# The low parts of w1 and w2 subtracted on VectorE instead of GpSimd, in a fused attention, gated product and soft mixture of experts

## The chip, the cores and the metric

One Trainium2 chip, one core of it. The time is that of one whole execution on the device in microseconds, as a median of runs. An execution with the hardware profiler is looked at beside it; its times are counted from the start of its span. The engines are TensorE (PE in the rows; PEld is its loading of weights), VectorE (DVE), ScalarE (ACT), GpSimd (POOL) and SyncE (SP, which issues most of the DMAs).

## The reference, cut to what matters

Attention with a causal mask and a decay bias over 32 heads of 576 tokens, a product of two projections in full precision, and a soft mixture of 8 experts. All inputs are float32.

```python
scores = scale * q @ k.T                      # 4 x 8 heads, 576 x 576, head_dim 64
scores = where(causal, -1e9, scores + minimum(bias, 0))   # bias from a cumulative sum of max(s, 0)
attn = exp(scores - max); attn /= sum(attn) + 1e-9
x = (attn @ v), heads side by side            # 2304 tokens x 512
a, b = x @ w1, x @ w2                         # w1, w2: 512 x 1024
x = (a * b @ w3) @ w_out                      # w3: 1024 x 1024, w_out: 1024 x 512
logits = x @ phi                              # 32 slots
slot_input = softmax over tokens(logits).T @ x
slot_out[e] = relu(slot_input[e] @ w1e[e]) @ w2e[e]
out = softmax over slots(logits) @ slot_out
```

## The kernel before, in words

The weights w1, w2, w3 and w_out come as 64-bit words of double precision and are turned into float32 on the chip. w1 and w2 together make eight tiles `w12t_0` to `w12t_7`, one for each block of 128 columns of the inner dimension; each comes in two halves of 512 words a partition (the names `w_w_5_1` and `raw_w_5_1` are the second half of tile 5). `fetch_words` has SP load a half into one of three buffers `raw` (L188). `load_words` then makes it a tile:

- ScalarE scales the high word (L202), VectorE shifts and ors in the sign and the low bits in three steps (L205, L206, L209). The last step, L209, is the last reader of the `raw` buffer, so the next SP load into that buffer waits for it.
- ScalarE rounds the float32 half to TensorE's reduced float32r (L233): the high part `th`. The difference between the value and its rounding is the low part `tl` (L234). A product with w1 or w2 is then the sum of three products of parts, `for wi, xi in ((0, 0), (0, 1), (1, 0))` at L457, so the matmuls of a block need both parts.

Around it, in the same stretch, runs the attention. For each head and tile of query rows TensorE makes scores in a PSUM buffer of the tag `sg` (L359; four such buffers, shared with the `gl` products of L457), VectorE adds the mask and takes the maximum (L362), ScalarE takes exponentials with their sum (L367), VectorE adds sums and inverts them (L376, L377), GpSimd scales the rows by the inverse (L380), TensorE transposes them (L395, L409) into PSUM buffers of the tag `tp` (two), ScalarE copies them out (L397, L411), TensorE multiplies with v (L110 with `x_ps`) and ScalarE and VectorE split the result into a rounded and a low part (L444, L445). As soon as x of a block is there, the `gl` products run, ScalarE copies one (L463) and VectorE multiplies it with the other (L475).

The order on the engines: the program is written as steps that `weave` mixes by costs, and a scheduler that simulates a timeline then lays out the instructions of TensorE, VectorE, ScalarE and GpSimd; each engine runs its own list in order. The order on SP stays as written. An operation that changes engine or length therefore changes the order around it, on all four engines.

Of the kernel before, what the change touches and what calls it, by code (L numbers as in the profile page):

```python
# [10 lines left out]
F32 = mybir.dt.float32  # L11
# [5 lines left out]
ALU = mybir.AluOpType  # L17
# [30 lines left out]
def attn_glu_softmoe_kernel(  # L48
# [14 lines left out]
    nc = tc.nc  # L63
# [127 lines left out]
    def convert(k, w, by_act, behind=None):  # L191
        raw = words.pop(k)
        pair = raw.bitcast(I32).rearrange("p (n t) -> p n t", t=2)
        hi, lo = pair[:, :, 1], pair[:, :, 0]
        wi, wu = w.bitcast(I32), w.bitcast(U32)
        order = mybir.DependencyInfo(mybir.DependencyClass.NoSync, mybir.DependencyReason.DATA)

        def line_up(step):
            if behind is not None:
                tc.add_manual_dep(step.ins, behind.ins.name, order, reason="order")  # L200

        line_up(nc.scalar.activation(out=w, in_=hi.bitcast(F32), func=AF.Copy, scale=F64_SCALE))  # L202
        lu = lo.bitcast(U32)
        if not by_act:
            nc.vector.tensor_scalar(out=wi, in0=wi, scalar1=3, scalar2=None, op0=ALU.logical_shift_left)  # L205
            nc.vector.scalar_tensor_tensor(  # L206
                out=wi, in0=hi, scalar=-0x80000000, in1=wi, op0=ALU.bitwise_and, op1=ALU.bitwise_or
            )
            return nc.vector.scalar_tensor_tensor(  # L209
                out=wu, in0=lu, scalar=29, in1=wu, op0=ALU.logical_shift_right, op1=ALU.bitwise_or  # L210
            )

        line_up(nc.scalar.activation(out=lo, in_=lu, func=AF.Copy, scale=LO_SCALE, bias=-0.49999))
        nc.vector.scalar_tensor_tensor(
            out=wi, in0=wi, scalar=3, in1=lo, op0=ALU.logical_shift_left, op1=ALU.bitwise_or
        )
        return nc.vector.scalar_tensor_tensor(
            out=wi, in0=hi, scalar=-0x80000000, in1=wi, op0=ALU.bitwise_and, op1=ALU.bitwise_or
        )
# [4 lines left out]
    def load_words(k, ap):  # L224
        (kind, i), e = TODO[k // 2], k % 2
        span = slice(512 * e, 512 * e + 512)
        if kind == "w12":
            if e == 0:
                w12_t[i] = wp.tile([P, 2, 2, KC, P], F32R, tag="W", name=f"w12t_{i}", bufs=NW)
            w = gq.tile([P, 512], F32, tag="g4", name=f"w_{kind}_{i}_{e}", bufs=NG4)  # L230
            convert(k, w, False)
            th, tl = (w12_t[i][:, n].rearrange("p a k f -> p (a k f)")[:, span] for n in range(2))
            nc.scalar.copy(out=th, in_=w)  # L233
            nc.gpsimd.tensor_tensor(out=tl, in0=w, in1=th.bitcast(F32), op=ALU.subtract)  # L234
        elif k < 2 * N0:
            if e == 0:
                rows_t[kind, i] = gq.tile([P, FC, P], F32, tag="g4", name=f"{kind}_{i}", bufs=NG4)
            rows_w[kind, i] = convert(k, rows_t[kind, i].rearrange("p c f -> p (c f)")[:, span], True)
        else:
            if e == 0:  # L240
                rows_t[kind, i] = ap.tile([P, 1024], F32, tag="words", name=f"w_{kind}_{i}", bufs=NRAW)
            convert(k, rows_t[kind, i][:, span], True, st["a_copy"])
# [514 lines left out]
    with tc.tile_pool(name="att", bufs=1) as ap:  # L757
# [11 lines left out]
            out=mask[:, S - P :], in_=mask[:, S - P :], pattern=[[-1, P]], base=0,  # L769
# [27 lines left out]
        def load(k):  # L797
            i = k // 2 - 1
            if FC <= i < N0:
                (sum_rows if k % 2 else use_rows)(*TODO[i])  # L800
            if k < 2 * N0:
                load_words(k, ap)
            if k + NRAW < 2 * N0:
                fetch_words(k + NRAW, ap)
# [10 lines left out]
        for i in range(N0, len(TODO)):  # L815
            more += [(1, lambda i=i: fetch_later(i)), (1, lambda: None)]
            more += [(1, lambda k=2 * i + e: load_words(k, ap)) for e in range(2)] + [(1, lambda: None)]
# [84 lines left out]
    for a in range(0, 4, 2):  # L902
        zt_ps = psum("tp", f"zt_ps_{a}")
        for c in range(2):
            nc.tensor.transpose(zt_ps[:, c * P : (c + 1) * P], z_acc[:, (a + c) * P : (a + c + 1) * P], ident)
        nc.vector.tensor_reduce(
            out=zt[:, a : a + 2], in_=zt_ps[:, : 2 * P].rearrange("p (c t s) -> p c s t", t=2, s=2 * NS),
# [233 lines left out]
```

## Time and profile before

| | us |
|---|---|
| runs without the profiler | 549.1, 550.09, 554.26 (median 550.09) |
| the profiled execution, its own time | 552.43 |
| its span, first to last instruction | 550.7 |
| TensorE busy in the span | 516.8 (94%) |
| VectorE, ScalarE, GpSimd busy | 329.0, 311.6, 130.6 |
| mean granted TensorE clock | 0.993 |

The profiled execution is 2.3 us above the median; 1.7 us of its time lie outside the span. A busy share says how much of a stretch an engine was inside an instruction, not that it was the limit there.

### The profile page before, as it was taken

What the parts mean: (1) busy time and instruction counts of PE and PEld (TensorE: products, weight loads), DVE (VectorE), ACT (ScalarE), POOL (GpSimd) and SP (SyncE); (2) the same over time, 40 slices, a digit from 0 to 9 for tenths busy, and PEclk for the clock granted to TensorE, in tenths of its full rate; (3) what the DMA queues carried; (4) which work ended last, traced back from release to release, by engine and by line L of the source; (5) the groups of instructions that cost most, each with busy time, mean ns of one, the idle gap of its engine ahead of it and who ended that gap; (6) DMA issues with size and microseconds to landing.
All of it is one profiled execution on the core that took longest, in us unless ns stands there. A gap on an engine that the chain in (4) does not pass through costs nothing.

```text
span 550.7 us, 11764 instructions
## 1 busy us (share of the span) xinstructions
PE 516.8 (94%) x4288; PEld 434.3 (79%) x4288; DVE 329.0 (60%) x1016; ACT 311.6 (57%) x845; POOL 130.6 (24%) x199
## 2 busy tenths in 40 slices
PE   2799899998999999999999999999999999989993
PEld 2567678877788898999989889899989999843452
DVE  7558787879987394866577668566630311252433
ACT  4567667687986674866577567558644211321222
POOL 4475563102454232110221311111310000000000
PEclk9999989999999999999999999999999999999998
DMA  5746973977673253563656537553514999689977
GB/s 147 235 146 193 280 223 128 292 259 269 218 253 102 73 161 113 169 201 133 194 170 211 173 99 208 176 172 114 167 44 137 413 411 376 241 293 423 420 295 241
DMA packets 38809, 118.03 MB, mean 214 GB/s; under 512 B 4224, under 2 KB 10560, under 8 KB 35296
## 3 DMA queue, kind: packets, MB, share of 16 engines
q1 hardware_dynamic: 36768, 113.60, 61.0%
q10 hardware_dynamic: 1984, 3.69, 2.4%
q8 instruction: 34, 0.56, 0.4%
q14 instruction: 23, 0.19, 0.1%
HBM read 102.11 MB, written 11.60 MB: 206 GB/s over the span
## 4 chain that ended last, share of the span: by engine, by line
PE 70%; DMA 13%; DVE 8%; ACT 4%; issue 2%; POOL 1%; SPq 0%; ACTq 0%; DVEq 0%; POOLq 0%
PE gl L457 31%; PE sc_ps L359 7%; PE x_ps L110 7%; PE pt_ps L395 5%; DMA raw_w<-in_w 5%; PE gn_ps L627 3%; PE o_ps L1042 3%; DMA raw_w3t<-in_w3t 3%; PE h_ps L1004 3%; PE ptd_ps L409 2%; PE z_ps L110 2%; DMA raw_wot<-in_wot 2%; DVE sc L362 1%; PE lg L110 1%; ACT sc L367 1%
## 5 line engine op out<-in xcount | busy, mean ns | idle before, releaser
L457 PE MATMUL gl<-x,w12t 128*128 128x320 f32 (+1 forms) x1536 | 237.7, 304 | 0.1
L457 PEld LDWEIGHTS gl<-x,w12t 128*128 128x128 f32 x1536 | 212.7, 190 | 7.4 <-issue 4.4
L380 POOL TENSOR_SCALAR sc<-sc,rinv 128x64 f32<-128x64 f32 (+4 forms) x160 | 101.1, 650 | 253.0 <-DVE rinv L377 85.7
L367 ACT ACTIVATE sc<-sc,nmax 128x64 f32<-128x64 f32 (+4 forms) x160 | 89.8, 563 | 31.4 <-DVE nmax L362 29.1
L362 DVE CUSTOM_DVE_ANT_0 sc<-sc_ps,mask 128x64 f32<-128x64 f32 (+4 forms) x160 | 65.0, 423 | 31.8 <-PE sc_ps L359 31.0
L397 ACT COPY pt<-pt_ps 128x128 f32<-128x128 f32 (+3 forms) x128 | 53.0, 426 | 34.1 <-PE pt_ps L395 25.1
L395 PE MATMUL pt_ps<-ident,sc 128*128 128x128 f32 x320 | 56.6, 286 | 5.5 <-POOL sc L380 3.2
L395 PEld LDWEIGHTS pt_ps<-ident,sc 128*128 128x128 f32 x320 | 38.4, 144 | 16.9 <-POOL sc L380 7.2
L463 ACT COPY a<-gl 128x256 f32<-128x256 f32 (+1 forms) x64 | 25.4, 398 | 46.0 <-PE gl L457 40.7
L359 PE MATMUL sc_ps<-qa 128*128 128x64 f32 (+1 forms) x144 | 46.4, 334 | 1.3 <-DVE gT L475 0.8
L110 PE MATMUL x_ps<-pt,v 128*64 128x256 f32 (+1 forms) x384 | 47.4, 358 | 0.0
L359 PE MATMUL sc_ps<-raw 68*128 68x288 f32 (+4 forms) x96 | 35.8, 516 | 11.6 <-DMA raw<-rows 9.8
L359 PE MATMUL sc_ps<-qb 68*128 68x64 f32 (+1 forms) x144 | 43.6, 306 | 0.9 <-DMA qb<-qa 0.9
L110 PEld LDWEIGHTS x_ps<-pt,v 128*64 128x64 f32 x384 | 33.5, 140 | 5.8 <-issue 1.0
L359 PEld LDWEIGHTS sc_ps<-raw 68*128 68x128 f32 x96 | 21.6, 265 | 16.9 <-issue 14.1
L202 ACT ACTIVATE w_w<-raw_w 128x512 f32<-128x512 f32 x32 | 21.6, 676 | 17.8 <-DMA raw_w<-in_w 17.7
L445 DVE TENSOR_TENSOR x<-x_ps,x 128x320 fp32r<-128x320 f32 (+1 forms) x32 | 14.1, 452 | 29.2 <-ACT x L444 29.2
L630 ACT COPY gn<-gn_ps 128x512 f32<-128x512 f32 x40 | 22.5, 584 | 15.5 <-PE gn_ps L627 15.1
L367 ACT ACTIVATION_READ_ACCUMULATOR sc<-sc,nmax 128x1 f32 x160 | 30.9, 193 | 0.0
L359 PEld LDWEIGHTS sc_ps<-qa 128*128 128x128 f32 x144 | 27.4, 190 | 3.6 <-DVE gT L475 1.3
L409 PE MATMUL ptd_ps<-ident,sc 128*128 128x128 f32 x160 | 25.9, 286 | 3.2 <-ACT pt L397 3.0
L359 PEld LDWEIGHTS sc_ps<-qb 68*128 68x128 f32 x144 | 27.4, 191 | 1.6 <-DVE v_sb L276 1.0
(180 smaller groups left out, 725.6 us busy)
## 6 DMA issues: line engine op xcount, KB each, us to landing
ew<-in_ew SPq DMA_DIRECT2D x27, 1024.0 KB
raw_w<-in_w SPq DMA_DIRECT2D x32, 512.0 KB
raw<-in_qk SPq DMA_DIRECT2D x24, 576.0 KB
v<-in_v SPq DMA_DIRECT2D x16, 576.0 KB
raw_w3t<-in_w3t SPq DMA_DIRECT2D x16, 512.0 KB
raw_wot<-in_wot SPq DMA_DIRECT2D x8, 512.0 KB
raw_wo<-in_wo SPq DMA_DIRECT2D x8, 512.0 KB
w_d<-w_w SPq DMA_DIRECT2D x8, 512.0 KB
```

The source lines that it names most:

```text
L110: mm = nc.tensor.matmul(out_, lhs, rhs, start=start, stop=stop)
L202: line_up(nc.scalar.activation(out=w, in_=hi.bitcast(F32), func=AF.Copy, scale=F64_SCALE))
L359: nc.tensor.matmul(pp[:r, : z - a], x[:, 0, q0 : q0 + r], x[:, 1, a:z], start=x is mul[0], stop=x is mul[-1])
L362: nc.vector.tensor_tensor_reduce(out=sc[:r, a:z], in0=pp[:r, : z - a], in1=hd["mask"][:r, m0 : m0 + z - a], scale=-0.125, scalar=3.0e38 if ...
L367: nc.scalar.activation(out=sc[:r, :W], in_=sc[:r, :W], func=AF.Exp, bias=nmax[:r, i : i + 1], scale=-1.0, accum_out=rsum[:r, i, 0:1],)
L380: nc.gpsimd.tensor_scalar(out=sc, in0=sc, scalar1=rinv[:, i : i + 1], scalar2=1.0, op0=ALU.mult, op1=ALU.mult)
L395: nc.tensor.transpose(tp[:, j * P : (j + 1) * P], sc[:, j * P : (j + 1) * P], ident)
L397: t["turned", i] = nc.scalar.copy(out=pt[:, p0 : p0 + step * (i - 1) + 1 : step], in_=tp[:, : i * P].rearrange("p (j q) -> p j q", q=P))
L409: nc.tensor.transpose(dg[:, p0 : p0 + P], t["sc"][:, c0 : c0 + P], ident)
L457: nc.tensor.matmul(acc[:, :nt], w12_t[fc][:, wi, n, kc], x_t[b, blk, kc][:, xi], start=k == 0, stop=k == 3 * KC - 1)
L463: st["a_copy"] = nc.scalar.copy(out=a_sb[:, :nt], in_=acc[:, :nt])
L630: st["turned", blk, k, h] = nc.scalar.copy(out=gn[:r, 4 * h : 4 * h + 4].rearrange("p c f -> p (c f)"), in_=tp[:r])
```

## The change

The sixteen subtractions of L234 are issued on VectorE instead of on GpSimd. Nothing else is written differently.

```diff
             nc.scalar.copy(out=th, in_=w)
-            nc.gpsimd.tensor_tensor(out=tl, in0=w, in1=th.bitcast(F32), op=ALU.subtract)
+            nc.vector.tensor_tensor(out=tl, in0=w, in1=th.bitcast(F32), op=ALU.subtract)
```

The scheduler lays the engines out anew. GpSimd's list goes from 201 to 185 rows and keeps the order of all the others; VectorE's goes from 993 to 1009, and its rows and those of TensorE and ScalarE are permuted in many places over the whole program. SP's list is the same.

On GpSimd, the piece of the difference around the scaling of the score tile `sc_802` (heads of the first batch, tiles of 448 and 576 columns):

```order
 L380 TENSOR_SCALAR sc_696<-sc_696,rinv_807 128x448
 L380 TENSOR_SCALAR sc_696<-sc_696,rinv_807 128x576
-L234 TENSOR_TENSOR w12t_761<-w_w_5_1_819,w12t_761 128x512
-L234 TENSOR_TENSOR w12t_879<-w_w_6_0_880,w12t_879 128x512
-L234 TENSOR_TENSOR w12t_879<-w_w_6_1_932,w12t_879 128x512
 L380 TENSOR_SCALAR sc_802<-sc_802,rinv_895 128x448
 L380 TENSOR_SCALAR sc_802<-sc_802,rinv_895 128x576
```

Three subtractions stood ahead of the scaling of `sc_802`; now nothing stands between it and the scaling before.

On VectorE, the same place of the program, before, from the product `gC_0_1` to the last step of the words of tile 7, first half:

```order
L475 TENSOR_TENSOR gC_0_1_841<-gl_0_1_1_828,a_0_1_784 128x320
L209 SCALAR_TENSOR_TENSOR w_w_6_1_932<-raw_w_6_1_769,w_w_6_1_932 128x512
L205 TENSOR_SCALAR w_w_7_0_988<-w_w_7_0_988 128x512
L376 TENSOR_REDUCE rinv_895<-rsum_95 128x2
L206 SCALAR_TENSOR_TENSOR w_w_7_0_988<-raw_w_7_0_826,w_w_7_0_988 128x512
L377 RECIPROCAL rinv_895<-rinv_895 128x2
L209 SCALAR_TENSOR_TENSOR w_w_7_0_988<-raw_w_7_0_826,w_w_7_0_988 128x512
```

And the changed kernel, from the same product on:

```order
L475 TENSOR_TENSOR gC_0_1_841<-gl_0_1_1_828,a_0_1_784 128x320
L234 TENSOR_TENSOR w12t_879<-w_w_6_0_880,w12t_879 128x512
L205 TENSOR_SCALAR w_w_7_0_988<-w_w_7_0_988 128x512
L206 SCALAR_TENSOR_TENSOR w_w_6_1_932<-raw_w_6_1_769,w_w_6_1_932 128x512
L376 TENSOR_REDUCE rinv_895<-rsum_95 128x2
L206 SCALAR_TENSOR_TENSOR w_w_7_0_988<-raw_w_7_0_826,w_w_7_0_988 128x512
L209 SCALAR_TENSOR_TENSOR w_w_6_1_932<-raw_w_6_1_769,w_w_6_1_932 128x512
L377 RECIPROCAL rinv_895<-rinv_895 128x2
L205 TENSOR_SCALAR w_w_7_1_1041<-w_w_7_1_1041 128x512
L445 TENSOR_TENSOR x_1_0_361<-x_ps_1_786,x_1_0_361 128x256
L209 SCALAR_TENSOR_TENSOR w_w_7_0_988<-raw_w_7_0_826,w_w_7_0_988 128x512
```

Between `gC_0_1` and the inversion of `rinv_895`, on which the scaling of `sc_802` waits, four rows stood before and six stand now, one of them a subtraction.

On VectorE, the piece of the difference at the last part of the scores `sc_696`, a few us earlier:

```order
 L362 ISA sc_696,nmax_695<-sc_ps_4_0_730,mask 128x288
 L362 ISA nmax_695 128x1
+L234 TENSOR_TENSOR w12t_664<-w_w_4_1_716,w12t_664 128x512
+L362 ISA sc_696,nmax_695<-sc_ps_4_1_733,mask,nmax_695 128x288
+L362 ISA nmax_695 128x1
 L205 TENSOR_SCALAR w_w_5_0_762<-w_w_5_0_762 128x512
 L206 SCALAR_TENSOR_TENSOR w_w_5_0_762<-raw_w_5_0_609,w_w_5_0_762 128x512
```

A subtraction now stands inside the score tile, between its last two parts (which have moved ahead of the words of tile 5). The rounding that it needs stands on ScalarE in the changed kernel here, behind two copies of transposes:

```order
L233 CAST w12t_664<-w_w_4_0_665 128x512
L411 COPY ptd_539<-ptd_ps_547 128x192
L397 COPY pt_588<-pt_ps_1_590 128x128
L397 COPY pt_588<-pt_ps_2_593 128x2x128
L233 CAST w12t_664<-w_w_4_1_716 128x512
```

The copy of `pt_ps_2_593` has moved ahead of this rounding; before, it stood behind it.

## Rows read from the trace of the kernel before

**Rows 1.** Stretches, core 0: start:end, length, busy us (count) by engine, PEclk, DMA, GB/s.

```profile
10.00:48.00 38.00, 33.16 (x127) 24.71 (x128) 22.76 (x92) 24.67 (x82) 19.27 (x30) 1.00 0.63 183
48.00:84.00 36.00, 32.63 (x216) 26.46 (x215) 30.43 (x66) 25.17 (x62) 22.58 (x18) 0.95 0.81 241
```

**Rows 2.** The same view in slices of 10 us, four of them.

```profile
70.00:80.00 10.00, 8.81 (x63) 7.17 (x62) 8.86 (x18) 6.47 (x14) 5.58 (x5) 0.95 0.73 221
80.00:90.00 10.00, 10.00 (x51) 8.38 (x51) 8.44 (x23) 9.37 (x21) 4.83 (x4) 0.88 0.40 132
...
140.00:150.00 10.00, 8.78 (x68) 7.24 (x68) 9.26 (x27) 9.19 (x27) 5.05 (x6) 1.00 0.62 199
...
200.00:210.00 10.00, 10.00 (x83) 9.43 (x84) 7.15 (x28) 6.45 (x22) 5.50 (x10) 1.00 0.58 181
```

**Rows 3.** Waits, 0 to 85 us: engine line <- releaser: us, times, longest.

```profile
POOL w12t L234 <- ACT w12t L233: 19.6, 6, 5.5
...
ACT w12t L233 <- DVE w_w L209: 6.1, 9, 1.5
...
PE pt_ps L395 <- POOL sc L380: 2.1, 2, 1.2
```

**Rows 4.** Stretches, the instructions of L234 on GpSimd alone: busy us (count).

```profile
10.00:48.00 38.00, 8.02 (x6) 1.00 0.63 183
48.00:84.00 36.00, 14.73 (x10) 0.95 0.81 241
```

**Rows 5.** The same view of L209 on VectorE alone.

```profile
48.00:84.00 36.00, 11.84 (x9) 0.95 0.81 241
```

**Rows 6.** The same view of L380 on GpSimd alone.

```profile
48.00:84.00 36.00, 8.01 (x8) 0.95 0.81 241
```

**Rows 7.** VectorE, L206: ns min/median/max, first and last start, shape.

```profile
L206 DVE SCALAR_TENSOR_TENSOR w_w<-raw_w,w_w x16: 672/694/1019, 8.1 to 78.4; 128x512 int32<-128x512 int32 x16
```

**Rows 8.** VectorE, L332, in the same view.

```profile
L332 DVE TENSOR_TENSOR qb<-raw,qa x24: 739/751/973, 99.9 to 380.1; 64x576 fp32r<-64x576 f32 x24
```

**Rows 9.** Timeline, 46 to 50 us: start, us, engine, line, [idle before <- releaser].

```profile
46.09 0.69 DVE L209 SCALAR_TENSOR_TENSOR w_w<-raw_w,w_w 128x512 uint32<-128x512 uint32 x1
...
48.00 1.66 POOL L234 TENSOR_TENSOR w12t<-w_w,w12t 128x512 fp32r<-128x512 f32 x1 [3.46 <-ACT w12t L233]
...
48.57 1.65 DVE L209 SCALAR_TENSOR_TENSOR w_w<-raw_w,w_w 128x512 uint32<-128x512 uint32 x1
```

**Rows 10.** Timeline, 73 to 80 us.

```profile
73.31 0.48 DVE L475 TENSOR_TENSOR gC<-gl,a 128x320 f32<-128x320 f32 x1
...
73.71 1.39 DVE L209 SCALAR_TENSOR_TENSOR w_w<-raw_w,w_w 128x512 uint32<-128x512 uint32 x1
...
75.02 0.41 DVE L205 TENSOR_SCALAR w_w<-w_w 128x512 int32<-128x512 int32 x1
...
75.36 0.15 DVE L376 TENSOR_REDUCE rinv<-rsum 128x2 f32<-128x4 f32 x1
...
75.83 1.46 POOL L234 TENSOR_TENSOR w12t<-w_w,w12t 128x512 fp32r<-128x512 f32 x1 [1.28 <-ACT w12t L233]
...
76.08 0.16 DVE L377 RECIPROCAL rinv<-rinv 128x2 f32<-128x2 f32 x1
...
77.27 2.48 POOL L380 TENSOR_SCALAR sc<-sc,rinv 128x448 f32<-128x448 f32 x2
...
78.66 0.68 PE L395 MATMUL pt_ps<-ident,sc 128*128 128x128 f32 x3 [1.19 <-POOL sc L380]
```

**Rows 11.** TensorE by line and shape, 10 to 45 us: count | busy us, mean ns.

```profile
L395 PE MATMUL pt_ps<-ident,sc 128*128 128x128 f32 x15 | 5.3, 439 | 0.9 <-POOL sc L380 0.9
```

**Rows 12.** The same group of the same view, 46 to 78 us.

```profile
L395 PE MATMUL pt_ps<-ident,sc 128*128 128x128 f32 x30 | 5.2, 283 | 1.9 <-ACT pt L397 1.9
```

## The prediction

> **What bounds the kernel now.** I read the stretches first. From about 80 us on TensorE is busy nearly all the time; the slice 200:210, with 10.00 of 10 busy, stands for most of what follows [rows 2]. The subtractions of L234 all lie before that, six in 10 to 48 us and ten in 48 to 84 us [rows 4]. So they can change the time only by how soon TensorE gets through its first 84 us: by its idle time there, 38 - 33.16 = 4.8 us in the first stretch and 36 - 32.63 = 3.4 us in the second [rows 1], and by its clock. The first 10 us are loads and decay rows and hold no subtraction.
>
> In both stretches I then look at who has room. VectorE is idle 38 - 22.76 = 15.2 us in the first but only 36 - 30.43 = 5.6 us in the second [rows 1]. That second stretch is where the change is decided; six operations more in the first are lost in its idle time.
>
> Last, the waits and the two timelines show how L234 bears on the others. GpSimd stood 19.6 us in six waits at the head of its list for the rounding on ScalarE [rows 3], and what was queued behind it, the scaling L380, waited along. And L234 slows VectorE: an L209 by itself took 0.69 us, the one that began 0.57 us into an L234 took 1.65 us and ended 0.56 us after that L234 did [rows 9].
>
> **What it removes.** GpSimd loses 8.02 + 14.73 = 22.75 us of work [rows 4]. Most of that is no gain: TensorE waited for the scaling only 2.1 us in two waits in this stretch [rows 3]. I price the larger. The inverse for `sc_802` ended at 76.08 + 0.16 = 76.24, but an L234 held GpSimd until 77.27, and TensorE began the transposes at 78.66 after 1.19 us idle [rows 10]. Without L234 the scaling could begin with the inverse, 1.03 us sooner, if the inverse came at the same time. It does not: between `gC_0_1` and the inverse VectorE now has a subtraction and two more steps of words. Counted from the end of gC at 73.79: 0.67 (L234, below) + 0.41 (L205) + 0.69 (L206) + 0.15 (L376) + 0.69 (L206) + 0.69 (L209, undisturbed) + 0.16 (L377) = 3.46 us, less about 0.08 us of overlap at each of seven borders (gC ran from 73.31 for 0.48, its follower began at 73.71), so 2.9 us, and the inverse is there at 76.7 [rows 7, 8, 10]. The scaling starts 0.6 us sooner: **-0.6 us**, with 0 and -1.0 as its ends.
>
> VectorE gets back the stretch of its own steps. The nine L209 in 48 to 84 us took 11.84 us, where nine of 0.69 would be 6.2: **5.6 us of VectorE's time** [rows 5, 9]. In the stretch before that there is nearly none. ScalarE's rounding waited 6.1 us in nine waits for L209 [rows 3], with copies of transposes behind it in its list; a part of the 5.6 comes out there. I take a tenth of it as TensorE's time, since TensorE's whole idle time in the stretch is 3.4 us and has several other causes: **-0.5 us**, ends 0 and -1.5.
>
> **What it adds.** Sixteen subtractions of two SBUF tensors on VectorE. The trace of before has no such row at 128x512. The nearest is L332, the same operation and output type at 576 columns: 751 ns, times 512/576 = 0.67 us. L206, two SBUF inputs at 512 columns, took 0.69 us as a median. I take 0.67 [rows 7, 8]. In 10 to 48 us that is 6 x 0.67 = 4.0 us into 15.2 us of idle time: nothing. In 48 to 84 us it is 10 x 0.67 = 6.7 us, against the 5.6 us that come back. VectorE is fuller there by 1.1 us out of 5.6 idle: **0 us**, with +1.1 as the end if all of it lands on the path. The cover is VectorE's idle time; should it be gone, every further us on VectorE delays L362 and the inverses, and TensorE with them.
>
> The subtraction still reads two SBUF tensors, and GpSimd still runs L380 in this stretch, 8.01 us of 36 in eight instructions of 1.0 us [rows 6]. If a subtraction meets one it can be held like that L209. At a share of 8.01/36 = 0.22 that is 10 x 0.22 x 1.0 = 2.2 us at most on VectorE, of which I leave 0 in the forecast for the idle time and keep +2.2 as an end. The Trainium skill (SBUF — State Buffer, Who interferes with whom) says that a VectorE instruction with two SBUF inputs and a GpSimd instruction that reads SBUF contend, and that whichever came later is blocked to the end of the other. The pair of rows with the 1.65 us agrees [rows 9]. By that rule moving the subtraction removes L209's opponent but leaves L380 as one for all four steps of a half; it is the second rival.
>
> What is moved is the one instruction, with no DMA of its own. New on VectorE is its wait for ScalarE's rounding. Queued behind it in the place inside `sc_696` is an L362, whose PSUM buffer TensorE needs again for scores or for gl; that is the first rival. SP's list does not change, and the loads that wait for L209 can go up to 0.6 us (5.6/9) sooner each, which I count as nothing because TensorE has its weights in time.
>
> **The sum.** -0.6 - 0.5 + 0 = -1.1 us. Against the profiled execution, 552.43 - 1.1 = 551.3. That execution lies 2.3 us above the median of 550.09; for the median I take 550.09 - 1.1 = **549.0 us**, no change that one would call one. A change of 1% is 5.5 us, about what a measurement of this kernel tells from none: its own three runs span 5.2 us.
>
> **The rivals.**
>
> *VectorE waits at the head of its list (slower).* The place: a subtraction between two parts of a score tile whose rounding stands behind copies of transposes on ScalarE, as in `sc_696`. GpSimd spent 19.6 us in six such waits, the longest 5.5 us [rows 3]; without it 14.1 us in five remain. VectorE comes to the subtraction with more work done ahead of it and waits less; half is 7 us. It decides once these waits exceed the 5.6 us of idle time. For it: L234 stands ahead of L362 in several places. Against: the scheduler has put other VectorE work between rounding and subtraction in most. 550.1 + 7 = 557 us.
>
> *The collision only changes partner (no change).* L380 blocks subtractions and L209 as priced: 1.1 + 2.2 = 3.3 us on VectorE, all of it on the path: 549.0 + 3.3 = 552.3 us. For it: GpSimd now runs its scalings as soon as the inverse is there, in the middle of VectorE's words.
>
> *TensorE's clock (faster).* The granted clock was 0.95 in 70:80 and 0.88 in 80:90 [rows 2]. Between the two levels of 1.2 and 2.4 GHz that is 1.0 + 2.4 us at the lower one, worth half: 1.7 us. The fall comes right behind the 1.19 us of idle time; if that shrinks the fall may go. Earlier, transposes occupied 5.3/15 = 0.35 us each in 10 to 45 us and 5.2/30 = 0.17 us in 46 to 78 us [rows 11, 12]: by their durations TensorE was at the lower level until about 45 us, though the granted clock in the row is 1.00 [rows 1]. TensorE's list is permuted in this stretch too. Were the rise to come 8 us sooner, up to 4 us of its work there would be saved, and as much lost the other way. With the fall gone and most of the 4 us: 549.0 - 1.7 - 3.3 = 544 us.
>
> *The later stretch is laid out anew.* Behind 110 us, as in 140:150 with TensorE at 8.78 and VectorE at 9.26 of 10 [rows 2], a new order can make waits or save them, some 2 us either way. It has no sign of its own.
>
> **How the numbers follow.** Forecast 0.57; the waiting VectorE 0.16; the changed partner 0.10; the clock 0.15; the later stretch 0.02. Faster by over 1% (below 544.6) takes the clock's case and a little: 0.17. Slower by over 1% (above 555.6) takes the first rival and a little: 0.17. Within 1%: 0.66. The range reaches down to the edge of the clock's case, 543.5, and up to where the first rival begins, 556.0; it holds the changed partner, and the spread of the runs of before.
>
> **What would show it.** Right, if the profile after has sixteen L234 on VectorE near 0.67 us, the nine L209 of the dense stretch near 0.69 us, the transposes of `sc_802` less than 1 us late, and TensorE idle 7 to 8 us between 10 and 84 us. The first rival would show as VectorE waiting for L233 by several us and TensorE waiting for PSUM behind L362. The second would show as L234 on VectorE well above 0.67 us beside an L380. The third would show in the granted clock between 70 and 90 us and in the durations of transposes before 45 us. I am wrong if TensorE's idle time in the first 84 us moves by more than 3 us.

## The result, and the profile after

The changed kernel takes 554.72 us (median of 8 runs, 554.15 to 558.01) against 550.99 for the kernel before (8 runs, 548.22 to 554.26): ratio 1.0077, 95% interval 1.0049 to 1.0105. It is slower by 0.8% (3.7 us between the medians, 4.2 by the ratio), where 1.1 us less was forecast. The profiled execution took 557.5 us with a span of 555.7, so it lies 2.8 us above its own median, as that of before lay 2.3 above its own at the time. All ratios and intervals are those on record, of undisturbed runs alone, and are not quotients of the two medians (here 1.0068), though close to them.

The instruction that moved does what was forecast. VectorE's rows of the line L234, which was GpSimd's [rows 4]; columns: ns min/median/max, first and last start, shape.

```profile
L234 DVE TENSOR_TENSOR w12t<-w_w,w12t x16: 679/688/1098, 12.1 to 93.9; 128x512 fp32r<-128x512 f32 x16
```

And L209, whose collision with L234 stood ahead [rows 5, 9], in the same view.

```profile
L209 DVE SCALAR_TENSOR_TENSOR w_w<-raw_w,w_w x16: 678/688/732, 9.9 to 88.8; 128x512 uint32<-128x512 uint32 x16
```

Sixteen subtractions at 0.69 us, one of them 1.10; no L209 above 0.73 where one took 1.65 before. GpSimd's work fell from 130.6 to 108.5 us, VectorE's grew from 329.0 to 332.0 only. The waits of the changed kernel from 0 to 85 us answer [rows 3]; columns: engine line <- releaser: us, times, longest.

```profile
ACT w_w L202 <- DMA raw_w<-in_w: 18.0, 12, 3.3
...
PE pt_ps L395 <- ACT ptd L411: 3.1, 2, 2.7
ACT w12t L233 <- DVE w_w L209: 3.0, 3, 1.4
...
PE pt_ps L395 <- POOL sc L380: 1.1, 1, 1.1
...
DVE w12t L234 <- ACT w12t L233: 0.8, 2, 0.6
```

VectorE waits 0.8 us for ScalarE's rounding where GpSimd had waited 19.6; ScalarE waits 3.0 us for L209 instead of 6.1; TensorE 1.1 us for the scaling instead of 2.1. Each of the three got better. What got worse is the first row: ScalarE's first step on the words, L202, waited 18.0 us in twelve waits for transfers, where the same view of the kernel before has nine:

```profile
ACT w_w L202 <- DMA raw_w<-in_w: 13.3, 9, 2.6
```

The stretches of the changed kernel, which answer [rows 1]; columns as there.

```profile
10.00:48.00 38.00, 32.86 (x120) 23.06 (x121) 26.71 (x99) 23.48 (x77) 13.84 (x24) 1.00 0.58 164
48.00:84.00 36.00, 31.04 (x168) 23.50 (x169) 22.25 (x58) 20.55 (x51) 4.24 (x6) 0.91 0.69 200
```

In 48 to 84 us TensorE was busy 1.6 us less than before, but got through 168 products instead of 216, and VectorE through 58 instructions instead of 66. VectorE's became shorter on average (0.38 us instead of 0.46), TensorE's longer (0.18 instead of 0.15; the mix of shapes differs): work comes later, and a part of TensorE's runs slower, as the timelines below show. Two slices answer [rows 2].

```profile
70.00:80.00 10.00, 7.27 (x31) 6.25 (x32) 6.97 (x17) 6.70 (x16) 0.81 (x1) 0.73 0.77 217
80.00:90.00 10.00, 10.00 (x68) 7.92 (x67) 8.52 (x20) 4.71 (x11) 2.31 (x2) 0.92 0.48 162
```

TensorE was idle 2.7 us in 70 to 80, and the clock granted there fell to 0.73, where it had been 0.95.

Where the delay begins is seen at TensorE's list. The kernel before, TensorE's timeline from 38 to 58 us: the `x_ps` row is the products of the second pair of heads (items 2 and 3; an item is one head with one block of its query rows), the `sc_ps` row the scores of item 8.

```profile
42.05 1.49 PE L110 MATMUL x_ps<-pt,v 128*64 128x256 f32 x7
...
44.37 2.10 PE L359 MATMUL sc_ps<-raw 68*128 68x448 f32 x6
```

The changed kernel, TensorE's timeline of the same stretch and of 60 to 84 us.

```profile
41.88 3.75 PE L359 MATMUL sc_ps<-raw 68*128 68x448 f32 x6 [0.57 <-DMA raw<-rows_d]
...
46.05 1.49 PE L110 MATMUL x_ps<-pt,v 128*64 128x256 f32 x8
...
69.87 0.71 PE L457 MATMUL gl<-x,w12t 128*128 128x320 f32 x3 [1.16 <-ACT x L444]
...
74.58 1.00 PE L395 MATMUL pt_ps<-ident,sc 128*128 128x128 f32 x4 [2.73 <-ACT ptd L411]
...
77.31 3.81 PE L457 MATMUL gl<-x,w12t 128*128 128x320 f32 x12
```

The scheduler, laying out the lists with sixteen VectorE instructions more, put the six products of item 8's scores ahead of the second pair's (and permuted much else). The same six took 3.75 us instead of 2.10: by that duration they now ran at the lower of TensorE's two levels, though the clock column reads 1.00 (last section). The pair came 4.0 us later. The two waits of 1.16 and 2.73 us come some 25 us after that.

SyncE's queue shows one link between the two. The kernel before, SyncE's timeline: the loads of v and the last load of words ahead of the first.

```profile
38.67 0.53 SPq L188 DMA_DIRECT2D raw_w<-in_w  x1
43.99 0.33 SPq L308 DMA_DIRECT2D v<-in_v  x1
...
52.76 0.33 SPq L308 DMA_DIRECT2D v<-in_v  x1
```

The same of the changed kernel.

```profile
38.97 0.53 SPq L188 DMA_DIRECT2D raw_w<-in_w  x1
48.01 0.33 SPq L308 DMA_DIRECT2D v<-in_v  x1
...
58.62 0.33 SPq L308 DMA_DIRECT2D v<-in_v  x1
```

There are two buffers for v. The load for items 6 and 7 needs the one that the second pair's products read last, so it goes out when they end, at 44.0 us before and 48.0 after. Eight loads of q, k, decay rows and words stand behind it in the same queue. In 4-us windows of the changed kernel (last columns: granted clock, DMA share, GB/s) the transfers cease:

```profile
44.00:48.00 4.00, 4.00 (x26) 2.62 (x25) 3.96 (x13) 2.05 (x5) 2.27 (x3) 1.00 0.00 0
...
56.00:60.00 4.00, 4.00 (x33) 3.02 (x33) 2.42 (x7) 2.43 (x7) 1.36 (x2) 1.00 0.13 31
```

The same windows of the kernel before:

```profile
44.00:48.00 4.00, 3.39 (x14) 2.30 (x15) 2.95 (x10) 3.06 (x9) 0.54 (x2) 1.00 0.65 179
...
56.00:60.00 4.00, 2.93 (x30) 2.24 (x30) 2.54 (x6) 1.38 (x4) 3.93 (x3) 1.00 0.92 293
```

The products of items 10 and 11, which I use as a mark below, began at 95.56 us instead of 90.36. TensorE's timeline of the kernel before:

```profile
90.36 1.51 PE L110 MATMUL x_ps<-pt,v 128*64 128x256 f32 x12
```

And of the changed kernel:

```profile
95.56 1.51 PE L110 MATMUL x_ps<-pt,v 128*64 128x256 f32 x12
```

The two profiled executions lie 5.1 us apart and the medians 3.7, so about 1 of these 5.2 us belongs to the executions and not to the change.

### The profile page after: what moved, and what is told of

Read it like the earlier page. It is cut to its first block, busy times and chain, and to the rows that moved or that the text cites. A ratio compares the mean times of both kernels' runs of the same rounds, so it can differ in the third digit from the quotient of the medians.

```text
span 555.7 us, 11755 instructions
## 1 busy us (share of the span) xinstructions
PE 522.6 (94%) x4288; PEld 436.7 (79%) x4288; DVE 332.0 (60%) x1032; ACT 312.2 (56%) x845; POOL 108.5 (20%) x183
## 4 chain that ended last, share of the span: by engine, by line
PE 78%; DMA 10%; DVE 7%; ACT 2%; issue 1%; SPq 1%; ACTq 0%; DVEq 0%
PE gl L457 35%; PE sc_ps L359 8%; PE x_ps L110 8%; DMA raw_w<-in_w 6%; PE pt_ps L395 6%; PE gn_ps L627 3%; PE ptd_ps L409 3%; PE o_ps L1042 3%; PE h_ps L1004 3%; PE z_ps L110 2%; DMA raw_w3t<-in_w3t 1%; PE lg L110 1%; DMA qb<-qa 1%; DVE sc L362 1%; PE y_ps L928 1%
## 5 line engine op out<-in xcount | busy, mean ns | idle before, releaser
L380 POOL TENSOR_SCALAR sc<-sc,rinv 128x64 f32<-128x64 f32 (+4 forms) x160 | 101.3, 652 | 299.0 <-DVE rinv L377 148.7
L359 PE MATMUL sc_ps<-raw 68*128 68x288 f32 (+4 forms) x96 | 40.5, 568 | 12.8 <-DMA raw<-rows 9.8
L359 PEld LDWEIGHTS sc_ps<-raw 68*128 68x128 f32 x96 | 23.0, 284 | 19.9 <-issue 15.3
L110 PEld LDWEIGHTS x_ps<-pt,v 128*64 128x64 f32 x384 | 31.9, 142 | 8.5 <-issue 2.9
L202 ACT ACTIVATE w_w<-raw_w 128x512 f32<-128x512 f32 x32 | 21.6, 677 | 20.4 <-DMA raw_w<-in_w 20.3
```

Source lines behind the costliest of these rows:

```text
L110: mm = nc.tensor.matmul(out_, lhs, rhs, start=start, stop=stop)
L359: nc.tensor.matmul(pp[:r, : z - a], x[:, 0, q0 : q0 + r], x[:, 1, a:z], start=x is mul[0], stop=x is mul[-1])
L380: nc.gpsimd.tensor_scalar(out=sc, in0=sc, scalar1=rinv[:, i : i + 1], scalar2=1.0, op0=ALU.mult, op1=ALU.mult)
```

## The experiments

To tell the order from the operation, most kernels carry the order of another. At the kernel's end a block adds order-only edges (an edge fixes which instruction comes first and adds no wait) between neighbours of a list; `LAY` holds the lists as numbers (cut here). What each experiment changes beside it is shown with it:

```diff
+    LAY = (
...
+    )
+    traced = list(nc.cur_bb.bb.instructions)
+    for row in json.loads(zlib.decompress(base64.b85decode(LAY))):
+        at, prev = 0, None
+        for d in row:
+            at += d
+            if prev is not None:
+                tc.add_manual_dep(traced[at], prev.name, order, reason="laid out")
+            prev = traced[at]
```

The table gives all kernels. The mark is the start of the products of items 10 and 11 (the row `x_ps<-pt,v 128x256 x12` near 90 us on TensorE) in the one profiled execution of each.

| kernel | median us (runs) | ratio to before | 95% interval | mark us |
|---|---|---|---|---|
| before | 550.99 (8) | 1 | | 90.36 |
| after | 554.72 (8) | 1.0077 | 1.0049 to 1.0105 | 95.56 |
| e1 VectorE, old order | 552.53 (12) | 1.0018 | 0.9986 to 1.0051 | 86.88 |
| e2 GpSimd, new order | 553.35 (12) | 1.0044 | 1.0014 to 1.0074 | 88.88 |
| e3 after, second pair first | 557.9 (6) | 1.0137 | 1.0096 to 1.0179 | 95.11 |
| e4 before, scores first | 558.68 (6) | 1.0128 | 1.0079 to 1.0177 | 94.74 |
| e5 VectorE, old head, new rest | 550.73 (12) | 0.9971 | 0.9947 to 0.9994 | 87.17 |
| e6 VectorE, new head, old rest | 557.85 (12) | 1.0073 | 1.0038 to 1.0108 | 92.59 |
| e7 after, more v | 549.27 (12) | 0.9943 | 0.9914 to 0.9973 | 88.73 |
| e8 before, more v | 549.0 (11) | 0.9956 | 0.9929 to 0.9982 | 86.19 |
| e9 after, ScalarE's list | 555.59 (8) | 1.0077 | 1.0049 to 1.0104 | 91.72 |
| e10 e4, more v | 552.52 (12) | 1.0008 | 0.9977 to 1.0039 | 89.14 |
| e11 e5, more v | 548.63 (12) | 0.9939 | 0.9915 to 0.9963 | 85.56 |
| e12 e5, subtracted twice | 556.63 (6) | 1.0092 | 1.0055 to 1.0128 | 93.14 |
| e13 after, v behind | 555.39 (12) | 1.0036 | 0.9992 to 1.0080 | 87.27 |
| e14 e12, more v | 554.47 (12) | 1.0045 | 1.0009 to 1.0081 | 93.00 |
| e15 e3, more v | 553.79 (12) | 1.0027 | 0.9997 to 1.0056 | 90.46 |
| e16 after, more v, laid anew | 556.75 (6) | 1.0118 | 1.0078 to 1.0157 | 95.80 |
| e17 before, more v, laid anew | 554.73 (6) | 1.0086 | 1.0053 to 1.0119 | 91.26 |

**e1 and e2: the operation or the order.** e1 is the changed kernel with the lists of TensorE, VectorE and ScalarE in the order of before (`LAY` is read from that kernel; the sixteen subtractions are free). e2 is the kernel before with the lists of the changed one.

> The subtraction on VectorE as in the changed kernel, but TensorE, VectorE, ScalarE and GpSimd keep the order of the kernel before, row for row; the sixteen subtractions are slotted in between VectorE's rows by the scheduler. Theory A (the loss is the permuted order, the operation itself costs nothing): 548 to 551 us, ratio to the kernel before 0.995 to 1.001, the v load of the third pair issued near 44 us and the transposes at full clock from about 46 us. Theory B (the time on VectorE costs, the order is innocent): 554 to 556 us, ratio 1.006 to 1.010, with waits of TensorE behind L362 or the inverses. Theory C (the clock of TensorE rises early or late by chance, neither matters): anything between, with runs as far apart as 5 us.

> The other way round: the subtraction on GpSimd as before, but TensorE, VectorE and ScalarE and the rest of GpSimd in the order of the changed kernel, row for row; the sixteen subtractions are slotted in between GpSimd's rows by the scheduler. Theory A: 554 to 557 us, ratio 1.006 to 1.012, the v load near 48 us and the clock of TensorE high only after 55 us. Theory B: 550 to 552 us, ratio 0.999 to 1.002. Theory C: anything between.

With the old order the subtraction on VectorE costs nothing that can be told from zero; with the new order the kernel is slower although GpSimd subtracts. The order costs. Both ratios fall between the bounds that theories A and B had set: e2 carries about half of the changed kernel's loss, and its interval reaches up to nearly all of it, so a part of the loss for the engine in the new order is not excluded.

**e3 and e4: one place in TensorE's list.** e4 moves the six products (three rows of the list, each of them two in a timeline) in the kernel before to where the changed kernel has them; e3 moves them back in the changed kernel. In short, by the names in the lists:

```diff
 e4: TensorE's list of the kernel before
+sc_ps_3_0_564 sc_ps_4_0_574 sc_ps_4_1_577   (six products, item 8)
 x_ps_0_392                                  (second pair)
-sc_ps_3_0_564 sc_ps_4_0_574 sc_ps_4_1_577
 e3: TensorE's list of the changed kernel
-sc_ps_3_0_564 sc_ps_4_0_574 sc_ps_4_1_577
 x_ps_0_392
+sc_ps_3_0_564 sc_ps_4_0_574 sc_ps_4_1_577
```

> The changed kernel with its own order on all engines, except that on TensorE the three score products of the first tile of the second block (sc_563) stand behind the product with v of the second pair of heads (x_ps_0_392) instead of ahead of it. Theory A in its narrow form (that one place delays the release of the v buffer, and SP's queue behind it): the v load is issued 1.5 to 2 us sooner than at 48.0, since the copy that the product needs ends near 43.9, and the time falls by 1.5 to 3 us, to 552 to 553 us. Theory A in its wide form (many small permutations): 554 to 555 us. Theory B: 554.7 us, unchanged.

> The kernel before with its own order on all engines, except that on TensorE the same three score products stand ahead of the product with v of the second pair, as they do in the changed kernel. Theory A, narrow: the v load moves from 44.0 to 46 us or later, and the time rises by 1.5 to 4 us, to 552.5 to 555 us. Theory A, wide: 551 to 552 us. Theory B: 551 us, unchanged.

That place alone makes the kernel before 1.3% slower. Undoing it doesn't help the changed kernel, and rather makes it worse (the two intervals overlap a little), although the load of v for items 6 and 7 went out at 45.39 us, 2.6 sooner. So the theory that this one place is the loss fell. TensorE's timeline of e3:

```profile
42.15 0.45 PE L395 MATMUL pt_ps<-ident,sc 128*128 128x128 f32 x1 [2.02 <-ACT pt L397]
...
45.29 3.78 PE L359 MATMUL sc_ps<-raw 68*128 68x448 f32 x6
...
51.63 0.90 PE L409 MATMUL ptd_ps<-ident,sc 128*128 128x128 f32 x3 [2.13 <-ACT pt L397]
```

The other engines' lists were laid out with the scores first. With the pair first, TensorE stands 2.02 and 2.13 us for ScalarE's copies, the scores still run at the lower level (3.78 us), and the load of v for items 8 and 9 goes out at 60.85 us, later than in the changed kernel.

**e5 and e6: which half of the order.** The lists change from one order to the other at places where both have done the same work, about 96 us. In short:

```diff
+C1 = dict(PE=288, ACT=131, DVE=158)   # places in the lists
+LAY: e5 before[:C1] + after[C1:],  e6 after[:C1] + before[C1:]
```

> The subtraction is on VectorE; the lists of TensorE, VectorE and ScalarE run in the order of the kernel before up to about 96 us (the first 288 TensorE instructions) and in the order of the changed kernel behind that. Theory H (the loss is made in the head, by the order there): about 551.5 us, ratio to before 0.998 to 1.004. Rival L (the later part's order carries it): about 554.7, ratio 1.005 to 1.010. If both halves carry a part: between, about 553.

> The other half: the order of the changed kernel up to about 96 us and that of the kernel before behind it, the subtraction on VectorE. Theory H: as slow as the changed kernel, about 554.7 us, ratio 1.005 to 1.011. Rival L: about 551.5, ratio below 1.004.

The whole loss is in the head: 1.0073 with the new head, 0.9971 with the old one, and the intervals lie apart. The new order of everything behind 96 us costs nothing that shows. The load of v for items 6 and 7 went out at 43.19 us in e5 and at 48.68 in e6.

**e7 and e8: more buffers for v.** v of items 4 to 7 gets the two gU buffers, idle at that time and as large as the five parts of v that these items need. Lists unchanged.

```diff
-            vt = ap.tile([P, 9, 2, D], F32, tag="v", name=f"v_{n}", bufs=VB)
+            if n in (5, 7):
+                vt = gu.tile([P, 5, 2, D], F32, tag="gU", name=f"v_{n}", bufs=2)
+            else:
+                vt = ap.tile([P, 9, 2, D], F32, tag="v", name=f"v_{n}", bufs=VB)
```

> The changed kernel with all its lists as they are; the values v of items 4 to 7 get two buffers of their own (the gU buffers, idle at that time), so that no load of v in the first 70 us waits for an earlier pair's products, and SyncE's queue doesn't stand still at 39.5 to 48 and 52.7 to 58.6 us. Theory S (the stand of SyncE's queue behind v carries the loss): back to about 551 us, ratio 1.003 or less, the transfers of 44 to 48 us no longer at 0. Rival K (TensorE's later rise to its higher clock carries it, whatever the loads do): the loads go out early and the time stays at 554 or more, ratio 1.005 or more, with the same six products of 448 columns still at 3.7 us at 42 and 52 us.

> Control: the same buffers for v in the kernel before, its lists as they are. Theory S: little to win there, where SyncE's queue stands still for 4.8 us only (39.2 to 44.0), ratio 0.995 to 1.002. If it wins as much as the changed kernel does by it (ratio 0.993 or less), the stand is a cost to both and not what sets them apart. Rival K: ratio 0.998 to 1.003.

e7 falls from 1.0077 to 0.9943 (7.4 us), e8 by 0.44% (2.4 us). With nothing standing behind v the two kernels, each with its own order, can't be told apart. SyncE's timeline of e7: the loads for items 6 to 9.

```profile
35.41 0.42 SPq L311 DMA_DIRECT2D v<-in_v  x1
...
44.84 0.61 SPq L311 DMA_DIRECT2D v<-in_v  x1
```

They were at 48.01 and 58.62. Its 4-us windows, where the changed kernel moved nothing:

```profile
44.00:48.00 4.00, 4.00 (x26) 2.58 (x24) 3.97 (x12) 2.05 (x5) 2.27 (x3) 1.00 0.66 224
```

And its TensorE, products of items 2 and 3, 4 and 5, 10 and 11:

```profile
46.10 1.49 PE L110 MATMUL x_ps<-pt,v 128*64 128x256 f32 x8
...
57.52 1.49 PE L110 MATMUL x_ps<-pt,v 128*64 128x256 f32 x8
...
88.73 1.51 PE L110 MATMUL x_ps<-pt,v 128*64 128x256 f32 x12
```

Up to 57.5 us e7 is no sooner than the changed kernel (46.05, 57.44), and by the 1.49 us of its eight products it is still at the lower level then. It makes up 6.8 us between there and the mark. In e8 the six scores of item 8 ran almost wholly at the higher level (the six after them took 1.89 us):

```profile
43.96 2.08 PE L362 MATMUL sc_ps<-raw 68*128 68x448 f32 x6
```

A rise near 44 us and one behind 57 us end in the same time. So the late rise of the clock (rival K in the expectation) is not what sets the two kernels apart; the late loads are.

**e9: the link through ScalarE.** In the changed kernel the two L202 that waited for words at 68.85 and 73.63 us held the copies behind them in ScalarE's list, and TensorE waited for these. ScalarE's timeline of the changed kernel, the second of them:

```profile
73.63 0.66 ACT L202 ACTIVATE w_w<-raw_w 128x512 f32<-128x512 f32 x1 [2.80 <-DMA raw_w<-in_w]
74.19 0.25 ACT L411 COPY ptd<-ptd_ps 128x128 f32<-128x128 f32 x1
```

The two moves, in short:

```diff
 ScalarE's list of the changed kernel
-w_w_5_1 (L202)
 x_0_0_3 (L444)
+w_w_5_1 (L202)
...
-w_w_6_0 (L202)
 ptd_8 (L411)
 pt_9 (L397)
+w_w_6_0 (L202)
```

> The changed kernel, with two moves in ScalarE's list alone: the L202 step that waited 0.62 us at 68.85 stands behind the L444 copy of x, and the L202 step that waited 2.80 us at 73.63 stands behind the L411 and L397 copies of item 9's transposes. Link theory (the late words cost what they do because ScalarE's list holds the copies behind the waiting step, and TensorE waits for those): TensorE's waits of 1.16 and 2.73 us and the granted clock of 0.50 at 76 to 80 us go, some 3 to 4 us less than the changed kernel, 550.5 to 552, ratio to before at most 1.003. Rival (the words themselves are what TensorE needs next, through w12t): the wait shows under another name a little later, and the time stays at 554 or more, ratio 1.005 to 1.010.

The link theory fell. TensorE's timeline of e9:

```profile
70.14 0.52 PE L395 MATMUL pt_ps<-ident,sc 128*128 128x128 f32 x3 [0.61 <-ACT pt L397]
...
84.57 0.55 PE L395 MATMUL pt_ps<-ident,sc 128*128 128x128 f32 x3 [1.75 <-POOL sc L380]
```

The waits of 1.16 and 2.73 us are gone, 0.61 is left of them, and 1.75 us came up elsewhere; the time is the changed kernel's, although the mark in the one profile came 3.8 us sooner. Taking the longest wait out of a trace took nothing out of the median; the execution that showed this wait lay 2.8 us above its median, so the typical run may not have had all of it.

**e10 and e15: the buffers in e4 and e3.** The diff of e7 on the kernels of e4 and e3.

> The kernel before with the three scores of item 8 ahead of the second pair's products, as in e4, and the two more buffers for v. Theory S (a place in TensorE's list costs by when it frees v for SyncE's queue): the cost of e4 is gone, time as e8's, ratio 0.994 to 1.000. Rival (the place costs by itself, in TensorE's own chain or by its clock): e8's gain and e4's loss add up, ratio 1.006 to 1.010.

> e3 (the changed kernel with the second pair's products ahead of the three scores, slower than all) with the two more buffers for v. Theory S: what e3 lost, with its third load of v at 60.85 us, goes: ratio 0.993 to 1.000. Rival (the list of TensorE no longer fits those of ScalarE and VectorE, and its waits of 2.02 and 2.13 us for ScalarE cost by themselves): 1.005 or more.

The buffers are worth 1.2% to e4 and 1.1% to e3, as 1.3% to the changed kernel, against 0.3 to 0.4% with the old head (e5 to e11, before to e8). They don't take everything: e4's place costs 1.3% without them and 0.5% with them (e8 to e10), and e3's move 0.6% without (1.0077 to 1.0137) and 0.8% with them (e7 to e15). What e3 lost by its move doesn't go through v. Both ratios lie between the bounds of the two readings.

**e11: the best version.** e5 with the buffers.

> The version put together from the parts that helped: the subtraction on VectorE, the order of before up to about 96 us and of the changed kernel behind it, two more buffers for v. If the gains of e5 (0.9971) and e7 (0.9943) add up: ratio 0.990 to 0.993, about 547. If they are the same gain (nothing stands still any more, in whatever order): 0.993 to 0.997, about 549.

0.9939, which is 3.4 us below the kernel before (0.0061 of 551.6; 2.0 to 4.7 by the interval). The gains of e5 and e7 don't add up, as if they were one gain. The intervals of e7, e8 and e11 overlap: the buffers are the gain that is shown, and what the engine or the order still adds beside them is not.

**e12 and e14: VectorE's time.** Each subtraction done twice, the second writing the same values.

```diff
+            again = nc.vector.tensor_tensor(out=tl, in0=w, in1=th.bitcast(F32), op=ALU.subtract)
```

> As e5 (subtraction on VectorE, head in the old order), and each of the 16 subtractions is done a second time on VectorE right behind the first, writing the same values: 10.9 us more of VectorE (16 times 0.68). If VectorE's time for the subtraction is covered, as the prediction counted it: ratio within 0.003 of e5's 0.997, so 0.995 to 1.001. If VectorE's time there lies on the path in part (theory B): ratio 1.003 or more, up to 1.016 if all of it counts.

> e12 (each subtraction done twice on VectorE, head in the old order) with the two more buffers for v. If the 1.2% that the second time cost went through later products and SyncE's stand behind v: back to 0.993 to 0.998. If VectorE's time itself lies on the path by then: the same 1.2% above e11, 1.004 to 1.009.

The second dose of 16 x 0.68 = 10.9 us cost 1.2% (6.7 us), and 1.1% with the buffers (e11 to e14, 5.8 us): VectorE's time lies on the path for the second dose (theory B), and little of it goes through v. The dense stretch of e12 (columns as in [rows 1]):

```profile
48.00:84.00 36.00, 30.75 (x206) 25.24 (x205) 34.02 (x81) 22.72 (x55) 9.49 (x8) 0.94 0.74 227
```

And the same of e5:

```profile
48.00:84.00 36.00, 33.34 (x233) 27.21 (x232) 32.65 (x80) 26.34 (x64) 9.69 (x9) 1.00 0.78 235
```

With one subtraction VectorE was busy 32.65 of 36 us in the dense stretch, so 3.4 us were left; with two, 34.02, and TensorE lost 2.6 us there. The second write also holds w12t's readers 0.68 us longer each, which this experiment doesn't separate.

**e13: what stands behind v.** No buffer more; each load of v one item later in SyncE's queue.

```diff
-            prep = [(0, lambda n=n: att_values(n + 1, ap))] if n + 1 < N else []
+            prep = [(0, lambda n=n: att_values(n, ap))] if n < N else []
```

> The changed kernel, no buffer more, its lists of TensorE, VectorE, ScalarE and GpSimd as they are; in SyncE's queue each load of v stands one item later, behind the next four or five loads (a row of decay, two of q and k, one or two of words) instead of ahead of them. A load of v still waits for the same products, but less stands behind it. Theory S (what costs is the other loads that stand behind the waiting one): ratio to before 0.995 to 1.003. Rival (it is v itself that comes too late, or the place in SyncE's queue doesn't matter): 1.005 to 1.010, or slower than that, since v now comes later still.

1.0036, with an interval from 0.9992 to 1.0080 that takes in both readings: inconclusive. The mark came early (87.27).

**e16 and e17: the buffers, and the lists laid anew.** The diff of e7, on the changed kernel and on the one before, without the block of `LAY`: the scheduler lays out its own order.

> The changed kernel with the two more buffers for v, its lists laid out by the scheduler with these in view (PE's list differs from the changed kernel's from place 46 on) and not held to any earlier order. If an order costs mainly by the stand behind v, any order does: ratio to before 0.992 to 0.998. If each new order is a draw of its own: anywhere from 0.994 to 1.012.

> The same for the kernel before, subtraction on GpSimd. The same two readings: 0.992 to 0.998 where the stand is what costs, anywhere up to 1.012 where an order is a draw. Beside e16 it says again what the change of engine alone is worth, each with the order that the scheduler gives it: within 0.004 of e16 if the engine costs nothing.

Both are slower than the kernel before, by 1.2 and 0.9%, on either engine. TensorE's timeline of e16:

```profile
49.61 1.50 PE L110 MATMUL x_ps<-pt,v 128*64 128x256 f32 x8
...
59.80 0.63 PE L460 MATMUL gl<-x,w12t 128*128 128x320 f32 x1 [3.59 <-ACT x L447]
```

Its new order has the second pair at 49.6 us, later than any other kernel here but e17 (50.7), and TensorE waits 3.59 us for a copy of x that stands in ScalarE's list behind an L202, which itself waited 3.51 us for its words. So each new order is a draw of its own, the second reading of the two. The buffers take away the stand behind v, not whatever else an order brings.

## Why the prediction was wrong

**What failed is what was counted as nothing.** The step is the paragraph on what is moved ("SP's list does not change, and the loads that wait for L209 can go up to 0.6 us (5.6/9) sooner each, which I count as nothing because TensorE has its weights in time") with the rival of the order, which was put behind 110 us, at 2 us "either way", and given 0.02. SyncE's list did not change, but when it moves on is set by TensorE's products through v's buffer, and these were permuted in the head. The time of one load set when eight others went out. The order of the head measured +0.7% against the kernel before (e6, 1.0073) and +1.0% against e5 (0.9971); the later stretch, where I had looked for it, nothing that shows (e6 beside the changed kernel, 1.0073 and 1.0077). The term "0" for what is moved should have been some 4 us.

**The sum itself was near.** -1.1 us is a ratio of 0.998. With the old order the same operation on VectorE measured 1.0018 (e1), whose interval begins just above that, at 0.9986, and 0.9971 in the old head alone (e5), whose interval takes it in; beside the buffers 0.9939 against 0.9956 (e11, e8). Its parts are in the waits, though in the new order: 2.1 to 1.1 us for the scaling (0.6 forecast), 6.1 to 3.0 us of rounding behind L209. One reading in it was wrong: ahead of the inverse of `rinv_895` VectorE has a subtraction and one more step of words, not two; the sum counts the rows as they stand and is not touched. The cover was VectorE's idle time, and e12 shows what the prediction said of it: with the cover nearly gone a further 10.9 us cost 6.7.

**The rivals.** The head of VectorE's list: refuted, 0.8 us of waiting instead of 7 or more. The collision with L380: refuted at its price. One subtraction of sixteen was long, by 0.4 us, beside a pair of L380 as that rival says, and the pair took 2.31 us where the three before it took 1.36 to 1.52; the changed kernel's timeline:

```profile
85.07 2.31 POOL L380 TENSOR_SCALAR sc<-sc,rinv 128x448 f32<-128x448 f32 x2 [14.26 <-DVE w_w L205]
...
86.82 1.10 DVE L234 TENSOR_TENSOR w12t<-w_w,w12t 128x512 fp32r<-128x512 f32 x1
```

The Trainium skill (SBUF — State Buffer, Who interferes with whom) has GpSimd's reads contend with VectorE's two-input instructions. The pair of rows with 1.65 us agreed [rows 9], and with the subtraction gone from GpSimd no L209 here was held so long (at most 0.73 us). The clock: it went the other way, with 0.73 granted in 70:80, and the rise at 57 us or later instead of 45 by the durations of the products; e7 shows that the late rise is not the cause by itself. The price of that rival, up to 4 us "lost the other way", is the size of the loss by luck only.

**My test for being wrong was blind.** It asked whether TensorE's idle time in the first 84 us moves by more than 3 us. It moved by 1.9 (8.2 to 10.1, where 7 to 8 was to show the forecast right). The delay was in busy time at the lower level and in work that came later, which idle time doesn't count; the start of a given product does. Among all nineteen kernels the mark and the ratio go together (correlation 0.86): all those at 1.007 or more have it at 91.2 us or later, and of those with it before 91 none is above 1.0044. It is one execution each; e14 (93.00, 1.0045) is off the line, and e9 has the changed kernel's ratio with a mark 3.8 us sooner. From the mark to the end of the span seventeen of the nineteen profiles take 460.0 to 462.4 us (e6 464.0, e13 465.6): most of what sets them apart is made ahead of the mark.

**What stays open.** Which reader of the late loads costs the time: ScalarE's hold was tried and fell (e9), and words that come early don't save a bad order (in e16 the last L202 was at 68.6 us, in the kernel before at 75.7). That it is the loads behind v and not v itself is read from the traces, not tested: in the profiles of before and after no instruction waits for a load of v (the one of 48.01 us is first used near 63), while L202 waits 18.0 us for words. e13, made to test it, didn't settle it. And what the rest of e3's, e4's, e16's and e17's orders cost by was read from waits, not tested.

## What to carry to other kernels

Where a scheduler orders the lists, moving one instruction to another engine is two changes: the operation's time, and a new order of everything that the scheduler touches. Price the second by what each in-order queue waits for and who releases it (here a buffer of v, read by products that moved 4 us), not by whether that queue's own list changed. Without the buffers every permuted head here cost something, 0.4 to 1.4% (the changed kernel, e2, e3, e4, e6, e9). To tell the two apart, hold the old order with order-only edges and run the new operation in it; the version to keep here is that one with the buffers (e11, 0.9939, though e7 and e8 are as good within their intervals), while buffers with an order left to the scheduler lost what they had won (e16, e17).

## What was not expected of the hardware

TensorE's lower level can last long without showing in the granted clock. The windows 40:44 and 44:48 of the changed kernel read 1.00, yet its six scores took 3.75 us from 41.88 on, and the same six 2.10 us from 44.37 on in the kernel before. In e9 the windows from 40 to 56 us read 0.50, and the same six took the same 3.75 us there. A window of e9, then its products:

```profile
40.00:44.00 4.00, 3.33 (x8) 1.85 (x7) 2.07 (x6) 2.54 (x8) 0.79 (x2) 0.50 0.59 157
```

```profile
41.20 3.75 PE L359 MATMUL sc_ps<-raw 68*128 68x448 f32 x6 [0.67 <-DMA raw<-rows_d]
```

When the changed kernel rose to the higher level could be read only from durations of one shape.
